# Attention and routed experts in one kernel: the values' copy given to ScalarE, and another order of the first microseconds

## The chip, the cores and the metric

The kernel runs on one core of one Trainium2 chip. The core has five engines that run side by side, each with a queue of its own: TensorE (PE in the profile; PEld is its weight load), VectorE (DVE), ScalarE (ACT), GpSimd (POOL) and SyncE (SP, which here issues DMAs). The metric is the device time of one execution in microseconds (us), lower is better. The time before is the median of three runs, 487.25 us (486.17 to 487.31).

## The reference, cut to what matters

```python
def _attn_ref(q, k, v):                       # 8 batches, 12 heads, 448 rows, 64 columns
    scores = scale * np.matmul(q, k.transpose(0, 1, 3, 2))
    scores = np.where(mask, -1000000000.0, scores)       # causal mask
    attn = np.exp(scores - np.max(scores, axis=-1, keepdims=True))
    attn = attn / (np.sum(attn, axis=-1, keepdims=True) + 1e-09)
    return np.matmul(attn, v)

def _moe_ref(x, w_gate, w1, w2, capacity):    # x: 3584 rows of 768; 8 experts, capacity 80
    logits = x @ w_gate
    expert_idx = np.argmax(logits, axis=1)
    gate_w = softmax(logits)[row, expert_idx]
    for e in range(8):
        tok_idx = the 80 rows of expert e with the largest gate_w
        h = np.maximum(x[tok_idx] @ w1[e], 0.0)
        out[tok_idx] = gate_w[tok_idx, None] * (h @ w2[e])
```

All rows of `out` that no expert takes are zero.

## The kernel before, in words

The kernel has two stages. The first, up to about 345 us, is the attention of all 8 batches with the choice of rows beside it. The second loads the experts' weights and multiplies the chosen rows by them.

**Pairs.** Two heads of 64 columns fill 128 partitions and make a pair; there are 48 pairs, six to a batch. Work on a pair is spread over three turns of the main loop. In turn i, TensorE multiplies the scores of pair i+1 at the turn's end (`sp`, L426, 18 products in halves of high and low 16-bit parts, and `sp` L433, three products for the last 64 queries), turns the exponentials of pair i-1 over (`tp`, L483, 16 transposes in four groups) and multiplies those of pair i-2 by the values (`xp`, L506, 16 products). The names in the profile are those of the tiles.

**A turn** has eight slots (L1039). VectorE takes the scores out of PSUM, adds the mask and finds the largest of each row (`ns` and `nb`, L445, seven times a pair). ScalarE takes each to its exponential (`prob`, L449, also seven) and copies three of the four groups of transposes out of PSUM (`PT`, L488); VectorE copies the fourth (three instructions). In slot 6 the finished product with the values is copied from PSUM to `xu` (L511, one instruction of 128x448 a pair), on VectorE. The first `ns` of the next pair comes after it in VectorE's queue. Each engine takes its instructions strictly in the order in which the program writes them inside `tc.manual_schedule()` (L986).

**PSUM.** Products other than the scores draw from one pool of four banks (`ps_g`), so a new `tp`, `xp`, `rt` or `rl` waits until the bank used four tiles earlier has been read.

**Thirds.** Queries and keys come in thirds of a batch, two pairs each. Each third is split into a high and a low 16-bit part (`qk`): casts L402 on VectorE for the first thirds and on GpSimd later, differences L370 on GpSimd, and `corner` copies (L375, GpSimd) that lay the last 64 queries of the two heads side by side. The third 0 is split by `split_third(0)`: `first_pair` at once (L380 on ScalarE, L381 and two L370 on VectorE, two corner copies on GpSimd), `second_queries` at once on GpSimd (L388, L370, two corner copies), the second pair's keys in slots 1 (`second_high`, L393 on ScalarE) and 3 (`second_low`, L370 on VectorE). Third 1 is split in slots 5 to 11 (two casts on VectorE, then three L370, two corner copies and a fourth L370 on GpSimd).

**The start of GpSimd's queue.** Ahead of its first corner copy GpSimd makes the identity and the mask, clears parts of the values' buffers (L142), clears two `corner` tiles (L171), makes eight tables of numbers (`numbers`, L258 to L276) and issues an indirect DMA (L1000) whose two rows of indices all lie outside, so that nothing is loaded.

**Work of a batch beside the pairs.** While a batch's pairs run, the batch before is turned to rows (`rt` L605, `xr` L624 on VectorE, stored to HBM), multiplied by the gate (`gp` L559, `gs` L564 on ScalarE, `lp`, `lg`, `logit`), and its best rows are merged with those of the batches before (`gt`, `own` L833, `larger` L835, `rm` L799, `rr` L858 and others). The slots of all this stand in the tables STEPS, EARLY, ROWS0 and ROWS1.

Of the kernel before, what the change touches and what calls it, by code (L numbers as in the profile page):

```python
# [7 lines left out]
F32 = mybir.dt.float32  # L8
F32R = mybir.dt.float32r
F16 = mybir.dt.float16  # L10
# [7 lines left out]
P = 128  # L18
DH = 64
# [28 lines left out]
def attention_then_moe(  # L48
# [12 lines left out]
    nc = tc.nc  # L61
    B, _, NP, S = qT.shape
    N, D = out.shape
# [19 lines left out]
    akeep = att.enter_context(tc.tile_pool(name="akeep", bufs=1))  # L83
    apool = att.enter_context(tc.tile_pool(name="att", bufs=2))
    turn_stack = ExitStack()
    ps_g = turn_stack.enter_context(tc.tile_pool(name="ps_g", bufs=4, space=PSUM))
# [50 lines left out]
    PH = NP // HB  # L137
# [23 lines left out]
    def part_of(t, rows, at, *dims):  # L161
        t = t[rows]
        return bass.AP(tensor=t.tensor, offset=t.offset + at, ap=[list(t.ap[0])] + [list(d) for d in dims])
    for t in flipped:
        nc.vector.memset(part_of(t, slice(QB, P), COL[0], [WPT, 2], [COL[1] - COL[0], 2], [1, QB]), 0.0)
        nc.vector.memset(part_of(t, slice(0, QB), COL[2], [WPT, 2], [COL[3] - COL[2], 2], [1, QB]), 0.0)

    corners = []
    for r in range(2):
        t = akeep.tile([P, 2, PH, P], F16, name=f"corner{r}")  # L170
        nc.gpsimd.memset(t, 0.0)  # L171
        corners.append(t)

    PACE = 1.28

# [185 lines left out]
    def split_third(h):  # L361
# [11 lines left out]
        def corner(x):  # L373
            for j, rows in enumerate((lo, hi)):
                nc.gpsimd.tensor_copy(corners[h % 2][rows, :, x, j * QB:(j + 1) * QB], both[rows, 0:2, x, 0:QB])  # L375
# [7 lines left out]
            sub(v, k_lo[:, x], kf[:, x], k_hi[:, x])  # L383
            corner(x)

        def second_queries():
            x = slice(1, PH)
            g.tensor_copy(q_hi[:, x], qf[:, x])  # L388
            sub(g, q_lo[:, x], qf[:, x], q_hi[:, x])
            corner(x)  # L390

        def second_high():
            nc.scalar.copy(k_hi[:, 1:PH], kf[:, 1:PH])  # L393

        def second_low():
            sub(v, k_lo[:, 1:PH], kf[:, 1:PH], k_hi[:, 1:PH])

        if h == 0:
            return [first_pair, second_queries], {1: [second_high], 3: [second_low]}
        e = v if h < HB + 1 else g  # L400
        low = lambda x, i: lambda: sub(g, both[:, x + 1, i], (qf, kf)[x // 2][:, i], both[:, x, i])
        return [lambda: e.tensor_copy(q_hi, qf), lambda: e.tensor_copy(k_hi, kf), low(0, 0), low(2, 0), low(0, 1),  # L402
# [89 lines left out]
    def values_group(pr):  # L492
# [15 lines left out]
                        pr.PT[:, j, n0:n0 + w], start=(c == 0), stop=(c == NT - 1))  # L508

        def after():  # L510
            pr.bt.read = nc.vector.tensor_copy(pr.xu[:, pr.p, :], pr.xp)  # L511
        return work, after

    NO = NT - 1
# [443 lines left out]
    def later_on(slot, stages, gap=1):  # L958
        for x, f in enumerate(stages):
            plan.setdefault(slot + x * gap, []).append(f)  # L960
        return slot + len(stages) * gap
# [24 lines left out]
    with tc.manual_schedule():  # L986
# [5 lines left out]
        load_values(0)  # L992
        nc.sync.dma_start(wg_sb, wg)

        numbers()
        none = const.tile([2, 1], I32, name="none")
        nc.gpsimd.memset(none, N)
        nowhere = const.tile([2, DH], F32, name="nowhere")
        nc.gpsimd.memset(nowhere, 0.0)
        nc.gpsimd.indirect_dma_start(  # L1000
            out=nowhere, out_offset=None, in_=w2.rearrange("e p c (g d) -> (e p c g) d", d=DH)[0:N, :],
            in_offset=bass.IndirectOffsetOnAxis(ap=none, axis=0), bounds_check=N - 1, oob_is_err=False)
        now, soon = split_third(0)
        for f in now:
            f()
        for k, fs in soon.items():
            for f in fs:
                later_on(k, [f])
        third_plan(1, 0)
        for x, f in enumerate(late_constants()):  # L1010
            later_on(LATE + x * SLOTS, [f])
# [1 line left out]
        for i, pr in enumerate(pairs):  # L1013
# [25 lines left out]
            for k in range(SLOTS):  # L1039
# [8 lines left out]
                        afters[x][0]()  # L1048
                if turns and k in COPIED:
                    turns[COPIED[k]][1]()  # L1050
                if values and k == XSLOT:
                    values[1]()
                if k < len(afters):
                    afters[k][1]()
                for f in plan.pop(i * SLOTS + k, []):
                    f()
                if k == SLOTS - 1 and i + 1 < n:
# [387 lines left out]
```

## Time and profile before

| | |
|---|---|
| median of three runs | 487.25 us (486.17 to 487.31) |
| the profiled execution | 487.09 us, of which 485.3 us is the span from the first to the last instruction |
| TensorE busy | 438.3 us (90%) |
| VectorE busy | 422.8 us (87%) |
| ScalarE busy | 373.2 us (77%) |
| GpSimd busy | 235.6 us (49%) |
| granted TensorE clock, mean | 0.999 of full |

Busy times are sums over stages that differ: a share of 77% over the whole says nothing of a stretch in which that engine has no gap. A row of the timeline gives start, duration, engine, line, operation, output and input, and in brackets the idle time of the engine before it and what ended it. A piece of the chain of waits gives start, duration, engine, tile and line; the chain is the one sequence of work and waits that ended last.

### The profile page before, as it was taken

How to read it: one execution, taken by the hardware profiler on the slowest of the kernel's cores; microseconds unless marked ns; L12 is line 12 of the kernel's file. 1: busy time of each engine (PE TensorE's matmuls, PEld its weight loads, DVE VectorE, ACT ScalarE, POOL GpSimd, SP SyncE). 2: the span in 40 equal slices, each digit the busy share in tenths (PEclk: the TensorE clock that was granted, in tenths of full speed). 3: DMA queues.
4: the chain of work that ended last, by engine and by line, in shares of the span. 5: the costliest groups of instructions: out<-in, count | busy, mean ns of one | idle time of the engine just before them, and what ended most of it. 6: DMA issues, size and time to landing. Idle time of an engine off the chain costs nothing.

```text
span 485.3 us, 15212 instructions
## 1 busy us (share of the span) xinstructions
PE 438.3 (90%) x5530; PEld 324.4 (67%) x5530; DVE 422.8 (87%) x1416; ACT 373.2 (77%) x1012; POOL 235.6 (49%) x366
## 2 busy tenths in 40 slices
PE   2899999999989998998999899988889989999894
PEld 1567666667656665765665576555558989999794
DVE  4888799799989979998998999899668999999991
ACT  4799888788858866875886687577486989999991
POOL 6967638248644823765283466430245255432201
PEclk9999999999999999999999999999999999999999
DMA  7454755655665553665455466429937999999941
GB/s 232 151 191 154 268 194 193 223 178 204 211 197 188 190 177 117 219 221 193 153 169 179 157 221 205 153 78 371 396 106 213 369 389 385 382 406 407 402 175 42
DMA packets 46667, 109.90 MB, mean 226 GB/s; under 512 B 5842, under 2 KB 23250, under 8 KB 45952
## 3 DMA queue, kind: packets, MB, share of 16 engines
q1 hardware_dynamic: 45392, 105.20, 61.9%
q0 software_dynamic: 1056, 3.51, 2.3%
q8 instruction: 43, 0.70, 0.6%
q14 instruction: 32, 0.26, 0.2%
q10 hardware_dynamic: 144, 0.23, 0.1%
HBM read 85.35 MB, written 23.99 MB: 225 GB/s over the span
## 4 chain that ended last, share of the span: by engine, by line
PE 65%; DVE 17%; ACT 8%; issue 4%; DMA 3%; POOL 2%; POOLq 0%; DVEq 0%; ACTq 0%
PE xp L506 16%; PE tp L483 11%; PE sp L426 11%; DVE ns L445 4%; ACT prob L449 4%; ACT PT L488 4%; PE rt L605 3%; DVE rm L799 3%; PE gp L559 3%; PE hp L1243 3%; PE op L1253 2%; PE op L1250 2%; PE op L1252 2%; PE hp L1252 2%; PE hp L1253 2%
## 5 line engine op out<-in xcount | busy, mean ns | idle before, releaser
L449 ACT ACTIVATE prob<-ns,nb 128x192 f32<-128x192 f32 (+3 forms) x336 | 177.7, 533 | 66.6 <-DVE nb L445 65.6
L445 DVE CUSTOM_DVE_ANT_0 ns<-sp,mask 128x192 f32<-128x192 f32 (+3 forms) x336 | 137.2, 440 | 4.8 <-PE sp L426 2.8
L483 PE MATMUL tp<-ident,prob 128*128 128x128 f32 x768 | 111.8, 279 | 3.2 <-DVE ro L787 1.6
L506 PE MATMUL xp<-PT,vt 128*64 128x448 f32 (+3 forms) x768 | 93.6, 386 | 6.7 <-ACT PT L488 4.3
L1174 DVE SCALAR_TENSOR_TENSOR wl<-wraw,wh 128x768 f16<-128x768 f32 (+1 forms) x98 | 97.3, 1058 | 2.3 <-POOL wl L1365 1.6
L370 POOL TENSOR_TENSOR qk<-qk,qk 128x448 f16<-128x448 f32 x93 | 95.6, 1042 | 6.8 <-DVE qk L402 3.6
L483 PEld LDWEIGHTS tp<-ident,prob 128*128 128x128 f32 x768 | 83.4, 141 | 15.6 <-issue 5.1
L488 ACT COPY PT<-tp 128x512 f32<-128x512 f32 x144 | 83.0, 577 | 13.3 <-PE tp L483 12.6
L1189 ACT ACTIVATE wh<-wraw 128x768 f16<-128x768 f32 (+1 forms) x98 | 85.0, 924 | 3.8 <-PE hp L1253 1.4
L506 PEld LDWEIGHTS xp<-PT,vt 128*64 128x64 f32 x768 | 51.0, 136 | 51.9 <-issue 24.1
L426 PE MATMUL sp<-qk 64*128 64x448 f16 (+2 forms) x864 | 72.6, 304 | 13.5 <-DVE nb L445 6.5
L1252 PEld LDWEIGHTS <-wh 128*128 128x128 f16 x668 | 66.7, 100 | 2.7 <-issue 2.6
L1253 PEld LDWEIGHTS <-wl 128*128 128x128 f16 x668 | 66.7, 100 | 2.3 <-issue 2.3
L1250 PEld LDWEIGHTS <-wh 128*128 128x128 f16 x668 | 67.1, 101 | 1.0 <-issue 1.0
L449 ACT ACTIVATION_READ_ACCUMULATOR prob<-ns,nb 128x1 f32 x336 | 65.2, 194 | 0.0
L1331 POOL DMA_INDIRECT out<-yo,idx x8 | 29.3, 3657 | 61.2 <-ACT yo L1328 58.1
L426 PEld LDWEIGHTS <-qk 64*128 64x128 f16 x864 | 37.4, 96 | 30.3 <-issue 10.1
L488 DVE COPY PT<-tp 64x256 f32<-64x256 f32 x144 | 43.6, 328 | 4.9 <-PE tp L483 2.9
L1253 PE MATMUL op<-hh,wl 128*128 128x80 f16 x324 | 37.1, 202 | 1.3 <-issue 1.3
L1250 PE MATMUL op<-hh,wh 128*128 128x80 f16 x324 | 37.1, 202 | 0.8 <-issue 0.6
L1252 PE MATMUL op<-hl,wh 128*128 128x80 f16 x324 | 37.1, 202 | 0.1
L1250 PE MATMUL hp<-xh,wh 128*128 128x80 f16 x320 | 36.2, 202 | 1.1 <-issue 1.0
(180 smaller groups left out, 674.6 us busy)
## 6 DMA issues: line engine op xcount, KB each, us to landing
wraw<-w SPq DMA_DIRECT2D x48, 384.0 KB
wraw<-w SPq DMA_DIRECT2D x30, 512.0 KB
out<-mask SPq DMA_DIRECT2D x56, 192.0 KB
qk<-k_t SPq DMA_DIRECT2D x23, 448.0 KB
qk<-q_t SPq DMA_DIRECT2D x23, 448.0 KB
vt<-v_t SPq DMA_DIRECT2D x24, 384.0 KB
xs<-xr SPq DMA_DIRECT2D x42, 192.0 KB
wraw<-w SPq DMA_DIRECT2D x5, 1536.0 KB
```

Of the source, the lines that this page charges most:

```text
L370: sub = lambda e, o, a, b: e.tensor_tensor(out=o, in0=a, in1=b, op=ALU.subtract)
L426: nc.tensor.matmul(pr.sp[t, j], a[rows, p, queries(t)], c[rows, p, FROM[t]:FROM[t] + WIDTH[t]], start=(x == 0), stop=(x == 2))
L445: nc.vector.tensor_tensor_reduce(out=ns, in0=pr.sp[x], in1=m, scale=-1.0 / 8.0, scalar=HUGE, op0=ALU.add, op1=ALU.min, accum_out=nb)
L449: nc.scalar.activation(pr.P[:, OFF[x]:OFF[x] + w], got[0], AF.Exp, bias=got[1], scale=-1.0, accum_out=pr.sums[:, h:h + 1])
L483: nc.tensor.transpose(tp[:, i * P:(i + 1) * P], f, ident)
L488: way(part_of(pr.PT, rows, to, *todims), part_of(got[0], rows, at, *dims))
L506: nc.tensor.matmul(xp[rows, c * P:S], st["vt"][:, c, p * P + j * DH:p * P + (j + 1) * DH], pr.PT[:, j, n0:n0 + w], start=(c == 0), stop=(c ...
L1174: return nc.vector.scalar_tensor_tensor(out=l, in0=src, scalar=SW, in1=h, op0=ALU.mult, op1=ALU.subtract)
L1189: nc.scalar.activation(h, src, AF.Copy, scale=SW)
L1250: nc.tensor.matmul(o, wh[:, ws], ah[:, c, :], start=(x == 0 and i % per == 0), stop=False, skip_group_check=True)
L1252: nc.tensor.matmul(o, wh[:, ws], al[:, c, :], start=False, stop=False, skip_group_check=True)
L1253: nc.tensor.matmul(o, wl[:, ws], ah[:, c, :], start=False, stop=(x == n - 1), skip_group_check=True)
```

## The change

It has five parts. The copy `xu` goes to ScalarE for all pairs but the last two, and in the loop the exponential of the slot is written ahead of it, so that on ScalarE it stands behind the pair's seventh exponential. The second pair of third 0 is split whole behind the first one: its keys' high part on ScalarE ahead of the exponentials, all the rest on GpSimd. This split is written ahead of the tables of numbers. The indirect DMA of L1000 with its two small clears goes to slot 12, that is slot 4 of the second turn. One corner tile is cleared by VectorE as its first instruction and the other by GpSimd behind the split; nine products of the zeros of the first corner tile (128x512, into a PSUM tile that nothing reads) stand at the head of TensorE's queue.

```diff
+    corners = []
+    for r in range(2):
+        t = akeep.tile([P, 2, PH, P], F16, name=f"corner{r}")
+        if r == 0:
+            nc.vector.memset(t, 0.0)
+        corners.append(t)
+    idle = ps_g.tile([P, 512], F32, name="idle", tag="g")
+    for _ in range(9):
+        nc.tensor.matmul(idle, corners[0][:, 0, 0, :], corners[0].rearrange("k x p q -> k (x p q)"), start=True, stop=True)
     for t in flipped:
         nc.vector.memset(part_of(t, slice(QB, P), COL[0], [WPT, 2], [COL[1] - COL[0], 2], [1, QB]), 0.0)
...
-    corners = []
-    for r in range(2):
-        t = akeep.tile([P, 2, PH, P], F16, name=f"corner{r}")
-        nc.gpsimd.memset(t, 0.0)
-        corners.append(t)
...
-        def second_queries():
+        def second_pair():
             x = slice(1, PH)
+            nc.scalar.copy(k_hi[:, x], kf[:, x])
             g.tensor_copy(q_hi[:, x], qf[:, x])
             sub(g, q_lo[:, x], qf[:, x], q_hi[:, x])
+            sub(g, k_lo[:, x], kf[:, x], k_hi[:, x])
             corner(x)
 
-        def second_high():
-            nc.scalar.copy(k_hi[:, 1:PH], kf[:, 1:PH])
-
-        def second_low():
-            sub(v, k_lo[:, 1:PH], kf[:, 1:PH], k_hi[:, 1:PH])
-
         if h == 0:
-            return [first_pair, second_queries], {1: [second_high], 3: [second_low]}
+            return [first_pair, second_pair]
...
-            pr.bt.read = nc.vector.tensor_copy(pr.xu[:, pr.p, :], pr.xp)
+            pr.bt.read = (nc.vector.tensor_copy if pr in pairs[n - 2:] else nc.scalar.copy)(pr.xu[:, pr.p, :], pr.xp)
...
+        for f in split_third(0):
+            f()
+        nc.gpsimd.memset(corners[1], 0.0)
         numbers()
         none = const.tile([2, 1], I32, name="none")
-        nc.gpsimd.memset(none, N)
         nowhere = const.tile([2, DH], F32, name="nowhere")
-        nc.gpsimd.memset(nowhere, 0.0)
-        nc.gpsimd.indirect_dma_start(
...
+        def first_gather():
+            nc.gpsimd.memset(none, N)
+            nc.gpsimd.memset(nowhere, 0.0)
+            nc.gpsimd.indirect_dma_start(
...
+        later_on(12, [first_gather])
...
+                if k < len(afters):
+                    afters[k][1]()
                 if values and k == XSLOT:
                     values[1]()
-                if k < len(afters):
-                    afters[k][1]()
```

ScalarE's queue from the fourth pair's exponentials of 448 columns to the fifth pair's second exponential, before (`prob` holds exponentials, `PT` the transposes that are copied out):

```order
L449 ACTIVATE prob_108,sums<-ns,nb 128x448 x2
L449 ACTIVATE prob_108,sums<-ns,nb 128x64
L449 ACTIVATE prob_107,sums<-ns,nb 128x192
L488 COPY PT_114<-tp 128x2x256
L449 ACTIVATE prob_107,sums<-ns,nb 128x192
```

The same place in the changed kernel, whose line numbers are one lower here:

```order
L448 ACTIVATE prob_108,sums<-ns,nb 128x448 x2
L448 ACTIVATE prob_108,sums<-ns,nb 128x64
L510 COPY xu<-xp 128x448
L448 ACTIVATE prob_107,sums<-ns,nb 128x192
L487 COPY PT_114<-tp 128x2x256
L448 ACTIVATE prob_107,sums<-ns,nb 128x192
```

The copy `xu` stands between the last exponential of one pair and the first of the next; on VectorE it stood between the last `PT` copy and the first `ns`.

GpSimd's queue from the clears of the values' buffers to the split of third 1, before (`qk_0` is the third 0, `qk_1` the third 1, `corner_119` and `corner_121` the two corner tiles):

```order
L142 MEMSET vt_111 64x256
L171 MEMSET corner_119 128x512
L171 MEMSET corner_121 128x512
L242 MEMSET tiny 128x1
L258 IOTA number 128x4
...
L276 IOTA slots_t 128x320
L997 MEMSET none 2x1
L999 MEMSET nowhere 2x64
L1000 DMA nowhere<-w,none 2x64
L375 COPY corner_119<-qk_0_125 64x2x64 x2
L388 CAST qk_0_125<-qk_123 128x448
L370 TENSOR_TENSOR qk_0_125<-qk_123,qk_0_125 128x448
```

The same engine and place in the changed kernel:

```order
L142 MEMSET vt_111 64x256
L245 MEMSET tiny 128x1
L378 COPY corner_115<-qk_0_134 64x2x64 x2
L392 CAST qk_0_134<-qk_132 128x448
L373 TENSOR_TENSOR qk_0_134<-qk_132,qk_0_134 128x448 x2
L378 COPY corner_115<-qk_0_134 64x2x64 x2
L996 MEMSET corner_117 128x512
L261 IOTA number 128x4
...
L279 IOTA slots_t 128x320
L373 TENSOR_TENSOR qk_1_135<-qk_133,qk_1_135 128x448 x3
L378 COPY corner_117<-qk_1_135 64x4x64 x2
L373 TENSOR_TENSOR qk_1_135<-qk_133,qk_1_135 128x448
```

The corner copies, the cast and the differences of the third 0 now come ahead of the tables, with one difference more, and the indirect DMA is gone from here to behind the fourth difference of third 1.

## Rows read from the trace of the kernel before

**Rows 1.** Busy time by stretch: the stretch, its length, busy us and instructions of each engine, the granted clock, the DMA engines' share and GB/s.

```profile
core 0: us, PE busy (x) PEld busy (x) DVE busy (x) ACT busy (x) POOL busy (x), PEclk, DMA share, GB/s
...
12.00:24.00 12.00, 10.48 (x85) 6.52 (x87) 10.65 (x42) 8.54 (x29) 11.46 (x16) 1.00 0.46 146
...
120.00:160.00 40.00, 36.95 (x368) 24.96 (x364) 35.95 (x151) 30.38 (x97) 21.08 (x38) 1.00 0.58 192
...
360.00:420.00 60.00, 56.24 (x1085) 52.89 (x1084) 56.13 (x70) 51.74 (x79) 28.32 (x11) 1.00 0.90 325
```

**Rows 2.** The chain of waits, the pieces of it that are the copy `xu` between 24 and 330 us: start, duration, what. There are nine; the first three and the last three stand here, and the three between (at 144.04, 187.50 and 230.96) are 0.53 us each.

```profile
66.15 0.53 DVE xu L511
...
72.18 0.60 DVE xu L511
...
100.57 0.53 DVE xu L511
...
274.43 0.53 DVE xu L511
...
317.90 0.53 DVE xu L511
...
324.63 0.62 DVE xu L511
```

**Rows 3.** Timeline, 134 to 149 us, VectorE, ScalarE and GpSimd, the rows around one of those copies.

```profile
137.33 0.19 DVE L833 TENSOR_TENSOR own<-gt,goh 128x32 f32<-128x32 f32 x1 [1.98 <-PE gt L812]
...
138.06 3.19 DVE L799 TENSOR_SCALAR rm<-slots_e,ro 80x80 bf16<-80x80 f16 x4
...
144.87 0.46 ACT L449 ACTIVATE prob<-ns,nb 128x192 f32<-128x192 f32 x1 [1.30 <-DVE nb L445]
...
138.04 3.02 POOL L370 TENSOR_TENSOR qk<-qk,qk 128x448 f16<-128x448 f32 x3
```

**Rows 4.** Groups of instructions by line over the whole span: busy us, mean ns of one, idle before and what ended it.

```profile
L511 DVE COPY xu<-xp 128x448 f32<-128x448 f32 x48 | 29.2, 609 | 4.8 <-PE xp L506 4.8
...
L564 ACT COPY gs<-gp 96x448 f32<-96x448 f32 x8 | 4.1, 515 | 3.1 <-PE gp L559 3.1
...
L488 ACT COPY PT<-tp 128x512 f32<-128x512 f32 x144 | 83.0, 577 | 13.3 <-PE tp L483 12.6
...
L1116 PE MATMUL wp<-before,identb 128*128 128x448 bf16 x39 | 8.7, 352 | 0.0
```

**Rows 5.** Timeline, 22 to 36 us, ScalarE and VectorE: the first exponential of two pairs (two turns apart), and the first and last `ns` of a pair.

```profile
21.70 0.45 ACT L449 ACTIVATE prob<-ns,nb 128x192 f32<-128x192 f32 x1
...
31.77 0.47 ACT L449 ACTIVATE prob<-ns,nb 128x192 f32<-128x192 f32 x1
...
25.63 0.36 DVE L445 CUSTOM_DVE_ANT_0 ns<-sp,mask 128x192 f32<-128x192 f32 x1 [0.23 <-PE sp L426]
...
28.25 0.08 DVE L445 DVE_READ_ACCUMULATOR2_ANT nb<- 128x1 f32 x1
```

**Rows 6.** The chain of waits in the first batch: the scores of the fourth and of the seventh pair.

```profile
24.72 1.33 PE sp L426 x18
...
40.27 1.33 PE sp L426 x18
```

**Rows 7.** Timeline of the first 20 us, all engines.

```profile
3.56 0.55 POOL L142 MEMSET vt<- 64x256 f32 x2
...
5.33 1.16 DVE L370 TENSOR_TENSOR qk<-qk,qk 128x448 f16<-128x448 f32 x2
...
6.47 0.42 POOL L276 IOTA slots_t<- 128x320 f16 x1
6.55 2.26 PE L426 MATMUL sp<-qk 64*128 64x192 f16 x14 [0.19 <-DVE qk L370]
...
7.33 1.14 POOL L1000 DMA_INDIRECT nowhere<-w,none  x1 [0.33 <-POOL nowhere L999]
7.82 0.36 DVE L445 CUSTOM_DVE_ANT_0 ns<-sp,mask 128x192 f32<-128x192 f32 x1 [1.33 <-PE sp L426]
...
11.65 0.29 POOL L375 COPY corner<-qk 64x128 f16<-64x128 f16 x1 [2.85 <-DMA nowhere<-w,none]
...
12.38 0.62 DVE L445 CUSTOM_DVE_ANT_0 ns<-sp,mask 128x448 f32<-128x448 f32 x1 [1.52 <-PE sp L433]
...
12.65 1.03 POOL L370 TENSOR_TENSOR qk<-qk,qk 128x448 f16<-128x448 f32 x1
...
13.07 1.72 DVE L402 CAST qk<-qk 128x896 f16<-128x896 f32 x2
...
13.74 2.42 PE L426 MATMUL sp<-qk 64*128 64x192 f16 x16 [0.78 <-POOL qk L370]
13.75 1.20 POOL L375 COPY corner<-qk 64x128 f16<-64x128 f16 x2
...
15.47 0.46 ACT L449 ACTIVATE prob<-ns,nb 128x192 f32<-128x192 f32 x1 [1.34 <-DVE nb L445]
...
17.09 0.59 ACT L488 COPY PT<-tp 128x512 f32<-128x512 f32 x1 [1.07 <-PE tp L483]
...
18.12 0.83 POOL L375 COPY corner<-qk 64x256 f16<-64x256 f16 x2
...
18.30 1.40 PE L426 MATMUL sp<-qk 64*128 64x192 f16 x18
```

More of the change, by code (lines that the diff above doesn't have):

```diff
@@ L993, in attention_then_moe @@
         nc.sync.dma_start(wg_sb, wg)
+        for f in split_third(0):
+            f()
+        nc.gpsimd.memset(corners[1], 0.0)
         numbers()
         none = const.tile([2, 1], I32, name="none")
-        nc.gpsimd.memset(none, N)
         nowhere = const.tile([2, DH], F32, name="nowhere")
-        nc.gpsimd.memset(nowhere, 0.0)
-        nc.gpsimd.indirect_dma_start(
[L1001 to L1008, printed above, removed]
+        def first_gather():
+            nc.gpsimd.memset(none, N)
+            nc.gpsimd.memset(nowhere, 0.0)
+            nc.gpsimd.indirect_dma_start(
+                out=nowhere, out_offset=None, in_=w2.rearrange("e p c (g d) -> (e p c g) d", d=DH)[0:N, :],
+                in_offset=bass.IndirectOffsetOnAxis(ap=none, axis=0), bounds_check=N - 1, oob_is_err=False)
+        later_on(12, [first_gather])
         third_plan(1, 0)
```

## The prediction

> **What bounds the kernel now.** The busy shares of the whole run say little, so I read the stretches first. From 120 to 160 us, the middle of the attention, TensorE is busy 36.95 of 40 us, VectorE 35.95 and ScalarE 30.38 [rows 1]: three engines near their limit, and 3 us of each 40 in which TensorE waits. What it waits for the chain of waits tells. In most pairs the chain runs along TensorE without a gap, and there nothing that other engines save counts. In one pair of each batch it leaves TensorE: VectorE waits for a product of TensorE (`own`, 1.98 us idle), then runs without a gap through `ns`, `rm` (3.19 us), `PT`, `rr` and the copy `xu` to the next pair's first `ns`, and ScalarE, idle for 1.30 us, starts that pair's exponentials when it has it [rows 3]. From there the chain returns over ScalarE to TensorE. So `xu` is on the path nine times [rows 2], of 48 copies in all.
>
> The start is another case. Here GpSimd decides: the second corner copy of the first pair stands behind the indirect DMA (1.14 us of issue) and waits 2.85 us more for it; VectorE waits 1.52 us for the products that need the corner, ScalarE 1.34 and 1.07 us [rows 7].
>
> **The sum is made against the profiled execution**, 487.09 us with a span of 485.3; it lies 0.16 us under the median of 487.25.
>
> **The copy leaves VectorE.** 46 of 48 copies of 609 ns [rows 4] go, 28 us of VectorE's time, but only the nine on the path count. Five of them (100.57 to 274.43) are the pair with `rm`, 0.53 us each. There the chain before is fixed by TensorE's product, and ScalarE idles 1.30 us behind it, so all of it is saved: 5 x 0.53 = 2.65. The other four (0.53 and 0.60 at 66 and 72, 0.53 and 0.62 at 318 and 325) sum to 2.28 [rows 2]; they stand in long stretches where TensorE is close behind, and I count 1.8. Together 4.45; bounds 2.0 (the path next to it ends halfway) and 4.95 (all nine, and nothing else).
>
> **The copy comes to ScalarE.** Its nearest rows are the copy of the same width, `gs`, 515 ns, and the wider `PT`, 577 ns [rows 4]; I take 0.51. It stands behind the pair's last exponential. Queued behind it are the next pair's exponentials, and for these TensorE waits. What covers it is the wait for the first `nb`: that needs new scores, which start only when `xp` is done, so an up-to-date ScalarE always idles there (1.30 us in rows 3). Hence nothing where TensorE or VectorE leads. Without that cover each copy costs 0.51. The first batch has no cover: ScalarE runs 5.03 us a pair there ((31.77 - 21.70) / 2) without a gap [rows 5], TensorE 5.18 ((40.27 - 24.72) / 3) [rows 6]; with the copy ScalarE needs 5.54 and becomes the slower one by 0.36 a pair, until the rows of the first batch make TensorE's turns longer. This counts in the next part.
>
> **The start.** VectorE's first difference is done near 5.9 (5.33 and half of 1.16). GpSimd is free at 4.1 (3.56 + 0.55) and copies the first corners from 5.9, 0.29 to 0.60 each, to 7.1 at the latest. The cast takes at most 0.7 (11.94 to 12.65), two differences 2.06, the second corners 1.20: the second pair's keys are complete at 9.9, its corner at 11.1. VectorE, which no longer waits for the corner (1.52) and no longer makes the second pair's difference, runs its seven `ns` in 2.7 (25.63 to 28.33) [rows 5] from 7.3 to 7.8 on, to 10.5 at the latest, then two casts, 1.72, and the second pair's first `ns`, 0.36: ScalarE starts that pair at 12.2 to 12.6, before at 15.47 [rows 7]. Without its wait of 1.07 it comes to the third pair at 17.4 (12.4 + 5.03), before 21.70 [rows 5]: 4.3 earlier. TensorE's limit is GpSimd: behind 11.1 come a clear and the tables (with the second clear at most 2.78 before, 4.11 to 6.89; I take 2.4), three differences 3.1, a corner 0.83: 17.4, where it was 18.95 [rows 7]. Three products, then 16 transposes and 16 products, back to back now since the exponentials are there: the period of 5.18 less the scores' 1.33 [rows 6], 3.85, so the fourth pair's scores at 21.3, before 24.72: 3.4 earlier. Does ScalarE then hold TensorE back in the first batch? It begins the seventh pair at 17.4 + 4 x 5.54 = 39.6 and has that pair's large exponentials at about 44.3; TensorE wants them two or so us after the eighth pair's scores, which stood one turn (5.18 or more) behind 40.27 and now stand 3.4 earlier, at 42.1 or later. That is just met, with no room.
>
> Against this stands the indirect DMA. It now follows third 1's last difference, at 18.4; if it again costs 1.14 + 2.85 [rows 7], GpSimd resumes at 22.6, while the fifth pair's scores (29.9 before, 26.5 now) need two differences of third 2 and their corner three and a copy: 3 x 1.03 + 0.83 = 3.9, and some small clears between. That is late by 0 to 1.0; I take 0.4. The nine idle products: 39 products of 448 columns take 8.7 us [rows 4], so 0.25 for 512 columns, and 0.44 at the pace of the first scores (2.42 for 16 against 1.40 for 18 later [rows 7]); 2.3 to 4.0 in all, while TensorE has nothing until 5.3. The granted clock reads 1.00 from 12 to 24 us [rows 1], the full level, though the products ran at little over half pace until 16 us; if the idle products bring the full pace for the first scores, 14 of which took 2.26, VectorE starts up to 0.5 earlier, if not nothing is lost; that is in the span from 7.3 to 7.8. Start in all: 3.4 - 0.4 = 3.0; bounds 1.0 and 4.3.
>
> One difference moves from VectorE to GpSimd and runs beside VectorE's casts. Rows show what such a pair can do: four `rm` took 3.19 us beside three differences of 3.02 [rows 3]. The Trainium skill says in GPSIMD Engine Reference, Key points, that GpSimd shares its SBUF interfaces with VectorE and contends with it in the modes that use both ports or with two inputs in SBUF. By that rule the two casts could stretch from 1.72 to the 3.3 us that GpSimd works beside them, and the start would bring 1.5 instead of 3.0, the whole 481.2. I keep 1.72, since these casts already ran beside a difference and two corner copies [rows 7].
>
> **Sum.** 487.09 - 4.45 - 3.0 = 479.6 us. What follows the attention keeps its own pace and moves as a whole (360 to 420 us: DMA share 0.90, TensorE 56.24 of 60) [rows 1], so what is won before it is kept.
>
> **Rivals.**
> First, the start alone: ScalarE's copies stand before exponentials that are just behind the chain, and the steady part is given back. For it: ScalarE is full in the first batch. Against: 1.30 us of idle time where it matters. 487.1 - 3.0 = 484.1.
> Second, the copies alone: the DMA's stall, now in the middle of a turn, and the first batch's full ScalarE eat the start. For it: the margin above is nil. 487.1 - 4.45 = 482.6.
> Third, more: the start brings 4.3, all nine copies 4.95, and VectorE's shorter turns free banks of PSUM sooner. 477.5 or a little under. Against: TensorE has no gap in most pairs.
> Fourth, slower: the copy waits in ScalarE's queue for TensorE's last `xp` product while the next pair's `nb` is ready, and holds every exponential behind it. The Trainium skill says in TensorE: Matmul & The Clock Gate, Architectural detail, that ScalarE takes its queue strictly in order, and the trace agrees: no exponential passes a `PT` copy that waits (1.07 us at 17.09 [rows 7]). At 0.51 a copy, 46 copies are 23 us; the mechanism outweighs the gains of 7.45 from 15 pairs on, and at 25 pairs it gives 492.4. Against: new scores start after `xp`, so `nb` cannot be ready first.
> Fifth, nothing: the freed VectorE waits for TensorE in the same turns and the start catches up by the first batch's end. 487.
>
> **How the numbers follow.** Forecast 0.55 (range of its own 477.5 to 482), start alone 0.14, copies alone 0.12, more 0.07, slower 0.06, nothing 0.06. About 0.3% (1.5 us) is what a measurement of this kernel can tell from no change. Faster: the first four, 0.88; same 0.06; slower 0.06. The range from 476.5 to 484.5 leaves out the last two and a little of the third.
>
> **What would show it.** In the profile after: ScalarE's first exponential of the third pair near 17.4, the fourth pair's scores near 21.3; no 2.85 us wait before a corner copy in the first 12 us; the idle products over by 5.4; `xu` on ScalarE near 0.51 and not in the chain outside the first batch; in the pair with `rm`, `rr` followed at once by `ns`, and batches 0.5 us shorter from about 90 us on. Wrong would be: ScalarE idle before `xu` and waiting for `xp` with `nb` at hand, exponentials in the chain turn after turn, or the fifth pair's scores waiting for GpSimd.

## The result, and the profile after

The changed kernel took 479.44 us in the median of four runs (477.9 to 480.6), the kernel before 487.13 us beside it (486.17 to 487.31): a ratio of 0.9844, with an interval from 0.9809 to 0.9879. The forecast was 479.6. The profiled execution shown below is the slowest of the four, 480.6 us with a span of 478.9. Two executions of one kernel below (the start alone) ran far longer than its others, 523.6 and 2363 us, and are left out of its time.

The same views as before, of the changed kernel (its line numbers differ by up to four from those before). First the busy time of the whole span and of the stretches of [rows 1].

```profile
PE 438.7 (92%) x5539; PEld 325.1 (68%) x5539; DVE 398.9 (83%) x1370; ACT 393.3 (82%) x1058; POOL 245.4 (51%) x366
```

```profile
12.00:24.00 12.00, 9.38 (x95) 6.53 (x94) 10.10 (x43) 11.35 (x39) 11.31 (x17) 1.00 0.49 141
120.00:160.00 40.00, 37.66 (x386) 25.37 (x383) 33.69 (x143) 32.37 (x104) 20.48 (x36) 1.00 0.54 179
360.00:420.00 60.00, 57.60 (x1184) 56.59 (x1185) 58.37 (x67) 53.60 (x83) 29.45 (x9) 1.00 1.00 363
```

In the middle of the attention VectorE fell from 35.95 to 33.69 us and ScalarE rose from 30.38 to 32.37, while TensorE, the engine that should be full, rose by only 0.7 us. VectorE's busy time over the whole span fell by 23.9 us (from 422.8 to 398.9); of that no more arrived than the path let through.

In the chain of waits the nine copies of [rows 2] are gone. Two new ones stand in it, on ScalarE; all pieces that are `xu`, up to 330 us:

```profile
39.02 0.41 ACT xu L510
...
63.64 0.41 ACT xu L510
```

The turn of [rows 3] in the timeline, 134 to 141 us: VectorE goes from `rr` straight to the next pair's `ns`, the copy runs on ScalarE beside `rr`, and ScalarE's wait for the first `nb` is 0.35 us where it was 1.30.

```profile
134.06 3.19 DVE L798 TENSOR_SCALAR rm<-slots_e,ro 80x80 bf16<-80x80 f16 x4
...
139.35 0.68 DVE L857 TENSOR_SCALAR rr<-slots_t,rank 128x80 bf16<-128x80 f16 x4
139.47 0.51 ACT L510 COPY xu<-xp 128x448 f32<-128x448 f32 x1
139.95 0.34 DVE L444 CUSTOM_DVE_ANT_0 ns<-sp,mask 128x192 f32<-128x192 f32 x1
140.34 0.46 ACT L448 ACTIVATE prob<-ns,nb 128x192 f32<-128x192 f32 x1 [0.35 <-DVE nb L444]
```

The groups by line (busy us, mean ns | idle before, released by), against [rows 4]: the copy takes 520 ns on ScalarE where it took 609 on VectorE, and VectorE's `ns` now waits 13.0 us for TensorE's scores, before 2.8 (the first row below is of the kernel before). That is where much of the freed time went.

```profile
L445 DVE CUSTOM_DVE_ANT_0 ns<-sp,mask 128x192 f32<-128x192 f32 (+3 forms) x336 | 137.2, 440 | 4.8 <-PE sp L426 2.8
...
L444 DVE CUSTOM_DVE_ANT_0 ns<-sp,mask 128x192 f32<-128x192 f32 (+3 forms) x336 | 137.4, 442 | 18.3 <-PE sp L425 13.0 <-ACT prob L448 3.1 <-ACT xu L510 1.9
...
L510 ACT COPY xu<-xp 128x448 f32<-128x448 f32 x46 | 23.9, 520 | 0.7 <-PE xp L505 0.4
```

The start in the timeline, against [rows 5, 7]: the first corner copies wait for VectorE's difference and no longer for the DMA, the tables end and the third pair's differences begin at 12.76, and ScalarE reaches the third pair at 16.71 where it was 21.70.

```profile
1.26 3.53 PE L172 MATMUL idle<-corner 128*128 128x512 f16 x9 [1.26 <-DVE corner L168]
5.75 0.87 POOL L378 COPY corner<-qk 64x128 f16<-64x128 f16 x2 [1.59 <-DVE qk L373]
6.18 1.23 PE L425 MATMUL sp<-qk 64*128 64x192 f16 x14 [0.27 <-DVE qk L373]
...
6.98 0.36 DVE L444 CUSTOM_DVE_ANT_0 ns<-sp,mask 128x192 f32<-128x192 f32 x1 [0.86 <-PE sp L425]
...
12.76 3.02 POOL L373 TENSOR_TENSOR qk<-qk,qk 128x448 f16<-128x448 f32 x3
...
16.71 0.44 ACT L448 ACTIVATE prob<-ns,nb 128x192 f32<-128x192 f32 x1
...
19.10 1.14 POOL L1004 DMA_INDIRECT nowhere<-w,none  x1 [0.33 <-POOL nowhere L1003]
20.26 0.30 POOL L293 CAST identb<-ident 128x128 bf16<-128x128 f32 x1
```

In the chain the fourth pair's scores start at 21.05 (24.72 in [rows 6]). But then the chain leaves TensorE in the first batch, which it did not do before: pieces of it, 34 to 44 us.

```profile
34.75 0.33 ACT prob L448
...
36.84 2.19 ACT prob L448 x8
39.02 0.41 ACT xu L510
39.44 0.37 ACT prob L448 x2
...
40.81 0.48 ACT PT L487
...
41.33 1.95 PE xp L505 x16
43.28 1.33 PE sp L425 x18
```

From 34.75 to 41.29 ScalarE works almost without a gap, and TensorE's product with the values waits for its last `PT` copy. This is where the copy has its price.

### The profile page after: what moved, and what is told of

It reads as the page before. It is cut to its first block, busy times and chain, and to the rows that moved or that the text cites. A ratio compares the mean times of both kernels' runs of the same rounds, so it can differ in the third digit from the quotient of the medians.

```text
span 478.9 us, 15257 instructions
## 1 busy us (share of the span) xinstructions
PE 438.7 (92%) x5539; PEld 325.1 (68%) x5539; DVE 398.9 (83%) x1370; ACT 393.3 (82%) x1058; POOL 245.4 (51%) x366
## 4 chain that ended last, share of the span: by engine, by line
PE 70%; DVE 14%; ACT 8%; issue 4%; POOL 2%; DMA 1%; POOLq 0%; DVEq 0%; ACTq 0%
PE xp L505 16%; PE tp L482 11%; PE sp L425 11%; DVE ns L444 4%; ACT prob L448 4%; ACT PT L487 3%; DVE rm L798 3%; PE rt L604 3%; PE hp L1242 3%; PE gp L558 3%; PE hp L1251 3%; PE op L1252 3%; PE hp L1249 3%; PE hp L1252 3%; PE op L1249 3%
## 5 line engine op out<-in xcount | busy, mean ns | idle before, releaser
L482 PE MATMUL tp<-ident,prob 128*128 128x128 f32 x768 | 110.3, 278 | 2.4 <-DVE ro L786 1.6
L505 PEld LDWEIGHTS xp<-PT,vt 128*64 128x64 f32 x768 | 51.0, 136 | 52.6 <-issue 23.9
L425 PE MATMUL sp<-qk 64*128 64x448 f16 (+2 forms) x864 | 71.0, 297 | 10.2 <-DVE nb L444 7.1
L1330 POOL DMA_INDIRECT out<-yo,idx x8 | 38.3, 4783 | 52.7 <-ACT yo L1327 49.4
L425 PEld LDWEIGHTS <-qk 64*128 64x128 f16 x864 | 36.9, 94 | 27.1 <-issue 12.1
```

Of the source, the lines that this page charges most:

```text
L425: nc.tensor.matmul(pr.sp[t, j], a[rows, p, queries(t)], c[rows, p, FROM[t]:FROM[t] + WIDTH[t]], start=(x == 0), stop=(x == 2))
L482: nc.tensor.transpose(tp[:, i * P:(i + 1) * P], f, ident)
L505: nc.tensor.matmul(xp[rows, c * P:S], st["vt"][:, c, p * P + j * DH:p * P + (j + 1) * DH], pr.PT[:, j, n0:n0 + w], start=(c == 0), stop=(c ...
```

## The experiments

The times of one kernel lie up to 2.7 us apart, more than some effects, so each trace is also read at three marks: the start of the scores of the fourth, the tenth and the forty-eighth (last) pair in the timeline (the chain of waits puts the same rows 0.06 us later). Between the tenth and the last pair lies the steady part. All in us:

| kernel | 4th | 10th | 48th | 4th to 10th | 10th to 48th |
|---|---|---|---|---|---|
| before | 24.66 | 58.55 | 331.93 | 33.89 | 273.38 |
| changed | 20.99 | 56.02 | 325.21 | 35.03 | 269.19 |
| changed, second trace | 21.78 | 56.55 | 325.80 | 34.77 | 269.25 |
| start alone | 20.83 | 54.74 | 328.24 | 33.91 | 273.50 |
| copies alone | 24.83 | 60.44 | 329.62 | 35.61 | 269.18 |
| DMA ahead | 26.32 | 61.76 | 331.01 | 35.44 | 269.25 |
| no idle products | 20.87 | 55.92 | 325.16 | 35.05 | 269.24 |
| first batch on VectorE | 21.08 | 54.98 | 324.15 | 33.90 | 269.17 |
| nine copies | 23.38 | 57.27 | 326.64 | 33.89 | 269.37 |
| copy ahead in its slot | 22.29 | 57.04 | 326.27 | 34.75 | 269.23 |
| tables first | 19.59 | 55.20 | 324.36 | 35.61 | 269.16 |
| gap filled | 26.10 | 59.99 | 329.17 | 33.89 | 269.18 |
| tables first, first batch on VectorE | 19.81 | 53.73 | 322.93 | 33.92 | 269.20 |

What comes behind the last pair's scores (the span less the third mark) took 151.8 to 153.7 us in these traces, 153.4 before and 153.7 in the first trace of the changed kernel; but for one copy `xu` and its place beside an exponential it is the same code in all.

### The two halves apart

The start alone:

```diff
-            pr.bt.read = (nc.vector.tensor_copy if pr in pairs[n - 2:] else nc.scalar.copy)(pr.xu[:, pr.p, :], pr.xp)
+            pr.bt.read = nc.vector.tensor_copy(pr.xu[:, pr.p, :], pr.xp)
...
-                if k < len(afters):
-                    afters[k][1]()
                 if values and k == XSLOT:
                     values[1]()
+                if k < len(afters):
+                    afters[k][1]()
```

> All 48 copies of the values' result back on VectorE, the start as changed. Theory (start and copies add up; the start brings 3.7 us at the fourth pair's scores, and what it loses on the way to the tenth pair is lost to a full ScalarE): without the copies on ScalarE the lead of 3.7 us is kept, the fourth pair's scores near 21.05, the tenth pair's near 58.62 - 3.6 = 55.0, the attention's end (the last gp transpose, 347.14 in the kernel before) at 343.5, and the whole 483.4 us. Rival (the lead is lost to something else in the first batch, such as GpSimd's later tables or its indirect DMA): the tenth pair's scores at 56.1 as in the changed kernel, the end at 344.6, the whole 484.5. Second rival (the start brings nothing by itself): 487.

> The start alone once more, for an undisturbed profile: all copies on VectorE, the start as changed. Theory (the lost lead of the changed kernel in its first batch is due to the copies on ScalarE): fourth pair's scores at 21.05, tenth pair's at 55.0, last gp products at 347.07 - 3.6 = 343.5. Rival (lost to something of the new start): tenth pair at 56.1, last gp products at 344.5.

Timed, it took 483.3 us in the median of five (482.94 to 485.17) against 486.67 (ratio 0.9941, 0.9923 to 0.9959). The marks are of the second of the two runs, a single execution of 481.95 us. The lead at the fourth pair, 3.83 us, is still 3.81 at the tenth and 3.69 at the last. So the new start loses nothing by itself in the first batch. That the changed kernel lost 1.14 us there has to do with the copies.

The copies alone, in the kernel before, is the reverse edit, with the start as it was.

> The kernel before with the copies on ScalarE and nothing else. Theory (the nine copies on the path count, about 4.2 us of them as measured between the tenth pair and the attention's end; the slow start leaves ScalarE no fuller than TensorE in the first batch, or costs up to 1 us there): the attention ends at 347.14 - 4.2 = 342.9, up to 343.9 if the first batch costs; the whole 483 to 484 us, and each pair with the row maximum 0.5 us shorter. Rival (ScalarE's copies hold back exponentials, and only the earlier start gave the gain): the end at 347 or later, 487 or more.

484.0 us against 486.67 (0.9946, 0.9933 to 0.9959). The steady part is 4.20 us shorter, as in the changed kernel. But the first batch costs 1.72, more than the 1 us allowed, so 2.31 are left at the last pair. Its chain, 28 to 46 us, goes back to ScalarE every second turn, with `xu` in it each time:

```profile
32.50 0.42 ACT xu L511
...
33.37 0.48 ACT PT L488
...
33.89 1.95 PE xp L506 x16
...
43.44 0.42 ACT xu L511
```

From the fourth to the seventh pair the scores come 5.47 us apart, where TensorE alone needs 5.18. The halves do not add up: 3.69 and 2.31 make 6.00, both together 6.72. The new start brought ScalarE to the third pair 4.99 us earlier and TensorE to the fourth only 3.67, so ScalarE has 1.3 us in hand that part of the copies' cost goes into. The kernel with the tables first (below) bears this out: ScalarE comes to the third pair at 16.64 there and TensorE to the fourth pair's scores at 19.59, 2.95 us later, as in the copies alone (21.88 and 24.83), and it pays the same from the fourth to the tenth pair, 35.61; the changed kernel, with 4.28 us between the two, pays 35.03.

### Whose copies count

First only the first batch's copies back on VectorE, then all but the nine of [rows 2]:

```diff
-            pr.bt.read = (nc.vector.tensor_copy if pr in pairs[n - 2:] else nc.scalar.copy)(pr.xu[:, pr.p, :], pr.xp)
+            pr.bt.read = (nc.vector.tensor_copy if pr in pairs[n - 2:] or pr in pairs[:6] else nc.scalar.copy)(pr.xu[:, pr.p, :], pr.xp)
```

> The changed kernel with the copies of the first six pairs back on VectorE, all others on ScalarE. Theory (in the first batch ScalarE has become the bound, each copy there costs its 0.41 us of pitch once its lead is used up): the lead of 3.67 us at the fourth pair's scores is kept, the tenth pair's scores at 55.0 (56.09 in the changed kernel), the last gp products at 339.25 (340.35), the whole 478.3 us. Rival (the lead is lost to TensorE or GpSimd, not to the copies): no difference, 479.4 us; or VectorE becomes the bound there and it is slower.

478.64 us against 486.77 (0.9839, 0.9821 to 0.9857). The first batch takes 33.90 us, the lead is kept, and the last pair's scores stand 1.06 earlier than in the changed kernel. The theory holds: 1.1 us of the new copy's cost is the full ScalarE of the first batch.

```diff
-            pr.bt.read = (nc.vector.tensor_copy if pr in pairs[n - 2:] else nc.scalar.copy)(pr.xu[:, pr.p, :], pr.xp)
+            pr.bt.read = (nc.vector.tensor_copy if pr not in [pairs[i] for i in (7, 8, 12, 18, 24, 30, 36, 42, 43)] else nc.scalar.copy)(pr.xu[:, pr.p, :], pr.xp)
```

> The changed kernel with only nine copies on ScalarE, those of the pairs whose copy stood in the chain of the kernel before; the other 39 on VectorE. Theory (only these nine count, and the first batch is freed of its copies): as the kernel with the first batch on VectorE, last gp products at 339.25, the whole 478.3 us, within 0.3 of that kernel. Rival (the shorter path comes from VectorE's lower load in all pairs, and copies that were just beside the path take the place of those taken off): last gp products at 340.5 to 343, the whole 479.5 to 482 us.

480.28 us against 486.77 (0.9866, 0.9851 to 0.9882). The whole looks like the rival, the marks say otherwise: the steady part is 269.37, 0.20 longer than with nearly all copies moved, so nine copies bring 4.01 of 4.2 us. And this with VectorE as full as without any change to the copies (the two rows are 120 to 160 us of this kernel and of the start alone):

```profile
120.00:160.00 40.00, 37.28 (x375) 24.97 (x376) 36.12 (x146) 30.78 (x99) 20.37 (x38) 1.00 0.57 187
```

```profile
120.00:160.00 40.00, 37.27 (x375) 24.63 (x374) 36.12 (x146) 29.40 (x95) 19.98 (x35) 1.00 0.53 178
```

The load that the other 39 copies put on VectorE did not matter; that these nine stood in the chain did. What this kernel lost, it lost ahead of the fourth pair, 2.3 us, in code that it shares with the one above; that is the matter of the clock below.

### The copy's place in ScalarE's queue

```diff
-                if k < len(afters):
-                    afters[k][1]()
                 if values and k == XSLOT:
                     values[1]()
+                if k < len(afters):
+                    afters[k][1]()
```

> The changed kernel with each copy on ScalarE ahead of the exponential of its slot in place of behind it. Theory (ScalarE takes its queue in order: the copy waits for the last product of the values, and with it the slot's exponential, though its negated maximum is there): every pair in which the values end behind that maximum loses up to a copy, 0.1 to 0.4 us a pair in the turns where ScalarE is on the path; the last gp products 1 to 6 us behind 340.35, the whole 480.5 to 485.5 us. Rival (the place in the slot does not matter, since the scores that ScalarE needs come behind the values anyway): 479.4 us, last gp products within 0.3 us of 340.35.

480.62 us against 486.77 (0.9881, 0.9861 to 0.99), the steady part 269.23: no difference from 269.19. The exponential that changes places with the copy is the pair's last and smallest (0.33 us). Of the 46 copies ten waited for the product, 5.6 us in all, where three had (2.6 us) behind the exponential; no mark shows a price of it. The loss of 1.3 us at the fourth pair lies again ahead of the first copies that could cause it.

### The parts of the start

The indirect DMA ahead of GpSimd's first casts and corner copies:

```diff
-        for f in split_third(0):
-            f()
-        nc.gpsimd.memset(corners[1], 0.0)
-        numbers()
...
-        later_on(12, [first_gather])
+        first_gather()
+        for f in split_third(0):
+            f()
+        nc.gpsimd.memset(corners[1], 0.0)
+        numbers()
```

> The changed kernel with the indirect DMA back ahead of GpSimd's first casts and corner copies; the rest of the start stays as changed. Theory (the wait is a written one: the first corner copy behind the DMA's issue waits until it lands): a corner copy of the first or second pair stands some 2.9 us again, the fourth pair's scores come 1 to 3 us later than 21.05, and the whole is 480.5 to 482.5 us. Rival (the DMA costs only its issue of 1.14 us on GpSimd, and no copy waits): the scores within 1.2 us of 21.05 and the whole within 1 us of the changed kernel's 479.4.

484.58 us against 486.67 (0.995, 0.9936 to 0.9963), with the fourth pair's scores at 26.32: worse than the theory, and worse there than the kernel before. GpSimd's timeline:

```profile
4.62 1.15 POOL L1000 DMA_INDIRECT nowhere<-w,none  x1 [0.34 <-POOL nowhere L999]
5.82 0.30 POOL L378 COPY corner<-qk 64x128 f16<-64x128 f16 x1
11.64 0.29 POOL L378 COPY corner<-qk 64x128 f16<-64x128 f16 x1 [5.52 <-DMA nowhere<-w,none]
```

Issued 2.71 us earlier than in [rows 7], it let the copy go at the same 11.64 as before (11.65). The wait of a corner copy for the DMA is real, and what ends it does not follow the issue. Moving the DMA behind these copies is what the new start lives from, though part of this price is the clock's (below), which read 0.50 from 13 to 21 us here. What the earlier split of the second pair and the moved clears bring by themselves was not run apart.

The tables back to where they were, ahead of the corner copies, and the DMA still late:

```diff
-        for f in split_third(0):
-            f()
         nc.gpsimd.memset(corners[1], 0.0)
         numbers()
+        for f in split_third(0):
+            f()
```

> The changed kernel with GpSimd's clear and tables back ahead of the first casts and corner copies; the indirect DMA stays behind them all. Theory (of the new order on GpSimd only the DMA's place counts; the tables cost the same 2.4 us wherever they stand ahead of the third pair): first corner copy near 6.9 us in place of 5.75, third pair's differences start near 12.8 us as in the changed kernel (12.76), fourth pair's scores at 21.05 +- 0.4, the whole 479.4 +- 0.6 us. Rival (the tables' place counts too): the fourth pair's scores 1 to 2.4 us later, the whole 480.5 to 482 us.

478.29 us against 486.55 (0.9834, 0.9815 to 0.9852): neither of the two. The tables' place counts, but the other way; the fourth pair's scores come at 19.59, 1.4 us earlier than with the tables late. GpSimd's timeline shows why:

```profile
6.00 0.42 POOL L279 IOTA slots_t<- 128x320 f16 x1
6.48 0.63 POOL L378 COPY corner<-qk 64x128 f16<-64x128 f16 x2
...
10.88 3.30 POOL L373 TENSOR_TENSOR qk<-qk,qk 128x448 f16<-128x448 f32 x3
```

Until 5.75 GpSimd had nothing else to do: in the changed kernel it idles 1.59 us there. The tables fill that hole, delay the first corner by some 0.7 us, and no longer stand in front of the third pair's differences, which begin at 10.88 and not at 12.76. ScalarE's full first batch then takes back 0.6 of it (35.61), and 0.85 is left at the last pair.

Without the nine idle products:

```diff
-    idle = ps_g.tile([P, 512], F32, name="idle", tag="g")
-    for _ in range(9):
-        nc.tensor.matmul(idle, corners[0][:, 0, 0, :], corners[0].rearrange("k x p q -> k (x p q)"), start=True, stop=True)
```

> The changed kernel without the nine idle products ahead of the first scores (they add nothing to the result). Theory (they bring the first scores to full pace): the first 14 products of the scores take 2.2 us again in place of 1.23, VectorE's first negated maximum comes 0.5 to 1 us later, and the fourth pair's scores 0 to 1 us later than 21.05, since GpSimd's chain limits them; the whole 479.4 to 480.4 us. Rival (the pace comes from elsewhere, and the idle products do nothing): 1.23 us for 14 products, and no difference at all.

479.77 us against 486.67 (0.9853, 0.9839 to 0.9867), all three marks within 0.12 us of the changed kernel. The first scores do slow down, as expected, and the first `ns` is 0.43 later than 6.98:

```profile
6.13 2.26 PE L422 MATMUL sp<-qk 64*128 64x192 f16 x14 [0.19 <-DVE qk L370]
...
7.41 0.36 DVE L441 CUSTOM_DVE_ANT_0 ns<-sp,mask 128x192 f32<-128x192 f32 x1 [1.32 <-PE sp L422]
```

GpSimd's chain to the third pair is longer and does not need them, so the idle products do what they can and bring nothing. Note that the granted clock reads 1.00 from 5 to 10 us in this trace as well as in the changed kernel's, though here the same products took nearly twice as long: in the first microseconds the pace of the products tells more than that column.

### The clock in the start, and the best version

> The changed kernel as it is, for a second trace and more times beside the two above. Theory (its four times went from 477.9 to 480.6 partly because the granted clock falls in its start in some executions): the whole 479.5 +- 0.8 us with a scatter of 2 us; if the clock falls in the profiled execution, the fourth pair's scores stand at 22 to 23.4 in place of 21.05 and the tenth pair's at 56.5 to 57.5. Rival (the scatter comes from what follows the attention alone): fourth pair's scores at 21.05 and a granted clock of 1.00 up to 30 us.

480.06 us against 486.55 (0.9871, 0.9854 to 0.9888). In this trace the fourth pair is 0.79 us later than in the first (a little less than the theory's 22), and the granted clock is below full; a value such as 0.82 is the mean of its two levels over the stretch. The busy time of 13 to 21 us, of this trace:

```profile
13.00:17.00 4.00, 2.14 (x16) 0.90 (x16) 2.20 (x12) 3.71 (x13) 3.81 (x5) 0.82 0.09 36
17.00:21.00 4.00, 4.00 (x28) 3.24 (x29) 3.94 (x15) 2.71 (x8) 3.62 (x6) 0.76 0.44 126
```

and of the kernel with nine copies, with its second pair's transposes at half pace and the first pair's values behind them slow as well (3.66 and 2.90 us, each 1.95 in the first trace of the changed kernel):

```profile
13.00:17.00 4.00, 1.70 (x21) 0.94 (x20) 3.56 (x17) 4.00 (x15) 3.81 (x6) 0.83 0.05 18
17.00:21.00 4.00, 4.00 (x21) 3.52 (x20) 2.93 (x10) 3.16 (x11) 3.58 (x7) 0.50 0.50 131
```

```profile
16.97 3.66 PE L482 MATMUL tp<-ident,prob 128*128 128x128 f32 x16
20.56 2.90 PE L505 MATMUL xp<-PT,vt 128*64 128x448 f32 x16
```

With the tables late, TensorE has little to do from 12.5 to 17 us, and in some executions its clock then falls to 0.50, the lower of its two levels (1.2 GHz); in others, as the first trace of the changed kernel, that of the start alone and that without idle products, it stays at 1.00. Of the nine traces with the tables late six show the fall, of the two with the tables first (below) neither; that the gap brings it on is argued from this count. What the fall costs is shown: with nine copies the two groups above took 2.66 us longer and began 0.26 earlier, and the fourth pair's scores came 2.39 later; with the copy ahead in its slot the transposes took 3.50, and the fourth pair came at 22.29. It need not cost much: in the kernel with the first batch on VectorE it read 0.69 from 13 to 17 us, and the fourth pair came on time.

The attempt to fill the gap, on top of the first batch's copies on VectorE (the dummies use the zeros of the second corner tile):

```diff
+    def fill(times, got={}):
+        if "b" not in got:
+            got["b"] = ps_g.tile([P, 512], F32, name="fill", tag="g")
+        for _ in range(times):
+            nc.tensor.matmul(got["b"], corners[1][:, 0, 0, :], corners[1].rearrange("k x p q -> k (x p q)"), start=True, stop=True)
...
+                    if pr is pairs[2] and t == 0 and x < 2:
+                        fill((5, 3)[x])
...
+            if pr is pairs[2]:
+                fill(5)
```

> The kernel with the first batch's copies on VectorE, and 13 dummy products of 512 columns (0.24 us each, into a bank that nothing reads) on TensorE where it waits for GpSimd between 12.5 and 17 us: five and three between the third pair's score products, five ahead of its corner products. Theory (TensorE's granted clock falls in some executions after this gap, to 0.50 of full speed for up to 4 us, which moves the fourth pair's scores from 21.05 to 22.3 and 23.4 in two of the traces): with the gap filled the granted clock reads 1.00 throughout the first 30 us, the fourth pair's scores are at 21.05 to 21.4 in every trace, the whole 478.2 us, and the runs scatter by under 1.2 us where those of the kernel without the dummies went from 477.88 to 480.22. Rival (the clock falls for another reason, or the dummies stand in the way): granted clock below 1.00 again, or the scores later than 21.8, and 479 us or more.

484.53 us against 486.55 (0.9958, 0.9944 to 0.9971), a miss of my making. The second corner tile is the one that GpSimd fills for the third pair, so the dummies waited for it and held up the scores behind them:

```profile
16.34 1.29 PE L177 MATMUL fill<-corner 128*128 128x512 f16 x5 [3.37 <-POOL corner L384]
```

On the clock it says little; after this longer wait it read 0.57 from 17 to 21 us. Whether dummies that wait for nothing keep the clock up was not tried. Tables first closes the gap with real work instead. Its trace, and that of the last kernel, which joins it with the first batch's copies on VectorE, read 1.00 throughout the first 30 us.

> The two edits that beat the changed kernel, in one: GpSimd's clear and tables ahead of the first casts and corner copies, and the first six pairs' copies on VectorE. Theory (the tables' place brings the fourth pair's scores to 19.6, and with no copies on ScalarE in the first batch this lead is kept, as it was between the fourth and the tenth pair of the kernel with the first batch on VectorE, 33.90 us): granted clock 1.00 up to 30 us, tenth pair's scores at 53.5, last gp products at 338.2, the whole 477.1 us. Rival (in the first batch GpSimd or VectorE is the next bound, and the earlier start is lost again): fourth pair at 19.6, but the tenth pair at 54.4 or later, the whole 478 us or more.

477.01 us against 486.82 (0.9809, 0.9789 to 0.9828), the tenth pair at 53.73, the last `gp` products at 338.07: as expected, and the fastest of all by the time and by the last mark (the changed kernel's two ratios are 0.9844 and 0.9871). Its chain from 30 to 54 us no longer leaves TensorE; three pieces of it:

```profile
33.54 1.88 PE xp L505 x16
35.42 1.33 PE sp L425 x18
36.75 0.19 PE sp L432 x3
```

## Why the prediction was right, point by point

**The nine copies.** The term was 4.45 us; 4.19 were measured, and moving the nine alone brings 4.01. The five beside `rm` gave 0.53 each, as priced. Of the other four, counted at 1.8, some 1.5 came. Pair by pair in the timelines, the lead over the kernel before grew by 0.49 and 0.44 at those of 66 and 72 us (0.53 and 0.60 in the chain), though ScalarE's own copy stands in the chain there at 63.64, and by 0.53 at that of 318. That of 325, 0.62 in the chain, gave 0.06: in its place the chain now runs through GpSimd's small steps, between the first row and the last:

```profile
317.58 0.10 DVE ggw L668
...
317.76 0.22 POOL ggw L676
...
320.12 0.41 PE selt L738 x4
```

**The copy on ScalarE.** 0.52 busy against 0.51 predicted, but 0.41 of pitch, since the next instruction starts before it ends. Outside the first batch it stands in the chain once, at 63.64, and costs nothing that the marks can show; the cover named, the wait for the first `nb`, is there.

**The first batch.** Here the argument failed in its size: "just met, with no room" was 1.14 us short. The pace of ScalarE, 5.47 us a pair in the copies alone, lies near the 5.54 predicted. But I let TensorE wait for the pair's large exponentials, and it waits for ScalarE's last `PT` copy, which stands behind them, the copy `xu` and the next pair's first ones. The lead of 3.67 us at the fourth pair (3.4 predicted) was 2.53 at the tenth.

**The indirect DMA.** The 0.4 us set against the start did not arise; in the trace the cast behind it follows at once (20.26). I took the wait for GpSimd's own; in the kernels that show it, it is a corner copy's. Behind the DMA's new place the next corner copy comes at 24.49, 5.4 us behind the issue, and by the trace the DMA took 5.4 us to land: no wait was left, but with nothing to spare, which I had not worked out. The two errors lie on opposite sides: 3.67 less 1.14 is 2.53, where the sum had 3.0.

**The idle products.** Over by 4.8, before the 5.4 asked for. Of my two cases the upper one came, full pace and VectorE's first `ns` 0.43 us earlier than without them; it is worth nothing at the fourth pair, since GpSimd is the limit there, as the sum had it.

**The difference moved to GpSimd.** The casts took 1.61, not 3.3 us, but the difference ran earlier, beside `ns`, whose 448 columns took 0.62 us there and 0.61 at 18.60 without it. What casts and differences do side by side the kernel with the DMA ahead shows:

```profile
12.64 2.40 POOL L373 TENSOR_TENSOR qk<-qk,qk 128x448 f16<-128x448 f32 x2
...
13.06 2.47 DVE L401 CAST qk<-qk 128x896 f16<-128x896 f32 x2
```

With the tables first the same casts took 1.26 us, mostly beside corner copies, and in the changed kernel two differences took 2.02. By the rule of the Trainium skill (GPSIMD Engine Reference, Key points) GpSimd contends with VectorE's instructions in modes that use both ports or with two inputs in SBUF. The trace agrees as far as these casts go, 2.47 us against 1.26; their mode it does not show. So my 1.72 was right for the changed kernel because its casts missed the differences, and not for the reason given: the 1.72 of [rows 7] beside a difference and two corner copies already held some of that price.

**Together** 6.72 us at the last pair's scores against 7.45. The rest of the median's 7.69 lies behind it, where traces of the same code differ by 1.9 us; that part of the agreement is luck. The second timing of the changed kernel gave 6.49 (486.55 to 480.06). Of the rivals, the start alone and the copies alone were each run and are worth 3.4 and 2.7 us by the times, 3.69 and 2.31 at the last pair's scores. The slower case did not occur in any kernel. Two slips in the sums, 481.2 for 481.1 and 12.2 for 12.1, change nothing.

## What to carry to other kernels

Move the instructions that stand in the chain of waits: here nine copies out of 46 brought 4.01 of 4.2 us, and the others cost 1.1 us where the engine that received them was full. Check an engine's load for the fullest stretch, not for the mean, before giving it work. And when an instruction is moved behind others to unblock them, look for the hole that it filled: the 2.4 us of tables cost 0.7 where GpSimd had to wait anyway, and held up the third pair by 1.9 where it did not.

## What the chip showed unexpectedly

TensorE's granted clock can fall in one execution and not in the next of the same program: between 13 and 21 us it read 1.00 in one trace of the changed kernel, 0.82 and 0.76 in another, and the fourth pair's scores moved by 0.79 us. The kernel before read 1.00 too, but its 16 score products at 13.74 took 2.42 us, where 18 took 1.40 later [rows 7]; so early in the program its column cannot be set beside the others.

The indirect DMA released the corner copy at 11.64 and 11.65 us though it was issued at 4.62 in one kernel and 7.33 in the other. From 5 to 10 us the first loads take 0.97 and 0.98 of the DMA engines in these two kernels; whether that holds it back was not tried.
